# Threshold and scores compared as bfloat16 views, and the program laid out anew: sparse attention with a feed-forward block, one Trainium2 core

## The chip, the core and the metric

One core of one Trainium2 chip runs the whole program. The metric is device time in microseconds; the kernel before took 1494.7 us (median of three runs, 1494.3 to 1497.42). Engines are named as in the profile: PE (matrix multiply, PEld its weight loads), DVE (VectorE), ACT (ScalarE), POOL (GpSimd), SP (which issues DMAs).

## What is computed

```python
scores = scale * np.matmul(q, k.transpose(0, 1, 3, 2))          # 8 batches, 8 heads, 576 x 576, D = 64
kth = np.partition(scores, -32, axis=-1)[..., -32:-31]
scores = np.where(scores >= kth, scores, -1e9)                  # only the 32 largest of a row stay
attn = np.exp(scores - scores.max(-1)); attn = attn / (attn.sum(-1) + 1e-09)
out = np.matmul(attn, v)
x = out.transpose(0, 2, 1, 3).reshape(4608, 512)                # tokens x model
h = x @ w_in                                                    # 512 -> 2048
g = s * np.maximum(h, 0) ** 2 + b
return g @ w_out                                                # 2048 -> 512
```

## The kernel before

**Attention** goes by tiles of 128 query rows by 576 keys: nine tiles for each pair of heads, 32 pairs, 288 tiles. For one tile PE makes the scores in two halves (`scores`, tile `s_ps`, one buffer), ACT copies them out (`sc`), and DVE looks for the 32nd largest of each row. It takes the eight largest of each of eight groups (`groups`), picks of these (`pick`, twice), negates (`negate`, tile `nt`), and takes the eight smallest candidates (`lowest`, tile `wl`). The last of those, `wl[7]`, is minus a threshold that is a little too low. `half_at` (POOL, line 458) turns its upper 16 bits, read as an integer, into a number between two steps of the upper half; `side` (ACT, line 464) compares the upper halves of all 576 scores with it by a Sign, and counts the signs with its accumulator. `window` and `pad` (POOL, tile `wt`) let only the scores below the threshold stand and fill as many pads as are to be dropped; `wmax` (DVE, tile `chk`) then finds the exact 32nd value, and `mask` (DVE) multiplies the exponentials `e` (ACT) with the comparison. PE transposes the result (`put`, tile `tp`), ACT and DVE split it into a high and a low part (`ph`, `pl`), and PE multiplies it with the values (`attend`, tile `av`). In the first batch the values are multiplied in one piece (lines 550 and 551), later in a high and a low part (lines 554 to 556).

**Feed-forward**: 18 blocks of 256 tokens, each with 16 chunks of 128 hidden units, 288 chunks. A chunk is 12 matmuls `h` (four channel groups of three), ACT's `relu` and `square`, POOL's `ghigh` and `glow`, and six matmuls `ops`. Block 0 needs the first four tiles of all four pairs of batch 0, that is the first 16 tiles, and each later block what its tokens need.

**Weights** come in 64 steps: DVE rebuilds float32 from the 64-bit words (three operations a step, `bits0` to `bits2`), ACT and POOL split it. Until the first `h` PE fills its idle time with matmuls that nobody reads (`keep_busy`, line 383).

**What sets the order.** All of this is one graph of operations. `PARTS` gives each kind its engine, how long it holds the engine (ns), how long until its result is there, and an offset to its priority. The priority (`key`) is the tile number plus the offset; a chunk's is `TURN0 + chunk / TURNS`, a weight step's `WTURN * n / 64`. `Graph.order` takes at each step, among what could start within `SLACK` ns of the earliest on an engine, the smallest key, and the instructions are issued in the order of the starts so planned, each engine's strictly in line. The number of `keep_busy` matmuls is 0.7 of PE's planned idle time before the first `h`, by 119 ns. At the end `flag0` reduces the thresholds of all tiles to a flag: if any is not positive, a slow general path computes everything again.

Of the kernel before, what the change touches and what calls it, by code (L numbers as in the profile page):

```python
# [40 lines left out]


PARTS = {
    "wload": ("SP", 1000, 4400, 8.71), "bits0": ("DVE", 325, 420, 38.47), "bits1": ("DVE", 330, 420, 12.33), "bits2": ("DVE", 322, 412, -54.81),
    "colsum": ("PE", 7400, 7600, -52.81), "far0": ("ACT", 322, 430, 45.58), "far1": ("ACT", 507, 524, -10.00), "far2": ("ACT", 782, 793, -41.40),
    "whigh": ("ACT", 322, 425, -19.96), "wlow": ("POOL", 702, 740, -54.59), "farmax": ("DVE", 170, 250, -9.09), "bias": ("ACT", 695, 700, -15.64),
    "kqload": ("SP", 1050, 4000, -31.15), "kqhigh": ("ACT", 574, 678, -31.99), "kqlow": ("POOL", 1389, 1430, -10.46),
    "kdir": ("SP", 560, 3800, -37.66), "kdhigh": ("ACT", 574, 678, -16.79), "kdlow": ("POOL", 1389, 1430, 9.70), "kdkeep": ("SP", 1100, 3600, -26.80),
    "qdir": ("SP", 500, 3400, -28.88), "qdhigh": ("ACT", 306, 405, 40.88), "qdlow": ("POOL", 694, 736, -38.25), "mdir": ("SP", 460, 2800, -9.58), "mdhigh": ("ACT", 170, 270, -53.70), "mdlow": ("POOL", 230, 280, -38.09),
    "kqkeep": ("SP", 1000, 3900, -48.58), "kplace": ("SP", 1000, 4400, -3.60), "qplace": ("SP", 480, 3000, -15.59), "mplace": ("SP", 500, 2400, 30.78),  # L50
    "vload": ("SP", 620, 3600, -16.48), "vhigh": ("ACT", 360, 466, 2.96), "vlow": ("POOL", 838, 875, 34.45), "vkeep": ("SP", 600, 2800, 48.38),
    "qk": ("PE", 132, 300, -43.54), "sc": ("ACT", 291, 408, -37.56), "group": ("DVE", 134, 218, 60.00),
    "m1": ("DVE", 86, 173, -57.06), "m2": ("DVE", 86, 173, 0.54), "neg": ("DVE", 95, 180, -1.22), "low8": ("DVE", 94, 180, 15.04), "max": ("DVE", 72, 160, -15.68),
    "half": ("POOL", 147, 190, 44.13), "side": ("ACT", 759, 860, -18.51), "win": ("POOL", 1250, 1290, -12.54),
    "exp": ("ACT", 667, 748, 55.25), "wmax": ("DVE", 668, 754, -35.90), "pad": ("POOL", 480, 420, -5.48), "mask": ("DVE", 731, 815, -58.93),
    "put": ("PE", 436, 680, 1.41), "putq": ("PE", 108, 350, 13.37), "high": ("ACT", 478, 595, 55.65), "low": ("DVE", 590, 675, -3.19),
    "resth": ("ACT", 264, 372, 17.15), "restl": ("DVE", 568, 610, -43.14), "av": ("PE", 146, 320, -18.63), "avout": ("ACT", 320, 470, -18.43),
    "eps": ("ACT", 95, 200, -14.34), "recip": ("DVE", 72, 180, 23.03),
    "sums": ("DVE", 140, 230, 34.96), "add": ("POOL", 1375, 1420, -57.27), "spread": ("POOL", 525, 560, -55.31), "turn": ("PE", 108, 352, -31.85),
    "scale": ("DVE", 325, 405, 11.38), "xkeep": ("SP", 500, 2600, 28.44),  # L60
    "xload": ("SP", 460, 2700, -54.47), "xhigh": ("ACT", 306, 405, -24.83), "xlow": ("POOL", 694, 736, -37.81),
    "h": ("PE", 357, 523, 40.36), "relu": ("ACT", 263, 378, -60.00), "square": ("ACT", 306, 415, -27.06), "ghigh": ("POOL", 369, 405, 56.67),
    "glow": ("POOL", 705, 745, 56.08), "o": ("PE", 231, 395, 42.40), "wagain": ("SP", 920, 3900, 44.77), "flag0": ("DVE", 560, 640, 60.00), "flag1": ("PE", 110, 360, 50.77), "flag2": ("DVE", 420, 500, 23.67), "osb": ("DVE", 654, 738, -13.89), "store": ("SP", 450, 2300, -30.67),
}
# [155 lines left out]
def fast_path(ctx, tc, kq, v, w_in, w_out, s_in, b_in, out, flag):  # L220
    nc = tc.nc
# [8 lines left out]
    scale = 0.125  # L230
# [19 lines left out]
    s_col, b_col, mid, cm, tm, tx, eps = (cols[:, x : x + 1] for x in range(PADS, PADS + 7))  # L250
# [41 lines left out]
    bias = const.tile([P, DM], F32, name="bias")  # L292
# [174 lines left out]

    def window(t):
# [263 lines left out]
    for i, (b, hp, pt, order) in enumerate(plan):  # L732
        pr = Pair()
# [10 lines left out]
        for n in order:  # L744
            t = TileState()
# [324 lines left out]
    for blk in range(NBLK):  # L1070
# [16 lines left out]
        for fc in range(NFC):  # L1087
# [246 lines left out]
```

## Time and profile before

| | |
|---|---|
| median of three runs | 1494.7 us |
| the profiled execution | 1495.7 us |
| its span, first to last instruction | 1493.9 us |
| mean granted PE clock | 0.986 |
| busy: PE, PEld, DVE, ACT, POOL | 1433.2, 1263.4, 1261.7, 1283.4, 1150.9 us |
| matmuls, keep_busy among them | 9468, 203 |

Busy is the time in which an engine has at least one instruction under way. Matmuls and the operations of DVE and ACT overlap the next one's start, so the mean of one is longer than what it holds its engine for: that is read from the starts of its neighbours.

### The profile page before, as it was taken

The page shows a single profiled execution, that of the slowest core. Times are in us where ns is not written, and L with a number is a line of the kernel's source. Part 1 is how long each engine was busy: PE and PEld are TensorE (multiplying, and loading weights), DVE is VectorE, ACT ScalarE, POOL GpSimd, SP SyncE. Part 2 cuts the span into 40 slices and gives each one's busy share as a digit, 9 for nine tenths or more (in the row PEclk, how much of TensorE's full clock was granted, in tenths as well). Part 3 has the DMA queues.
Part 4 walks back from the last instruction along what each step waited for, and adds up shares of the span by engine and source line. Part 5 has one row for each costly group of instructions (what it writes and reads, how often), then busy time and mean ns, then how long its engine had stood idle before and what let it go on. Part 6 is the DMA issues. An engine that isn't in the chain of part 4 may idle for free.

```text
span 1493.9 us, 34308 instructions
## 1 busy us (share of the span) xinstructions
PE 1433.2 (96%) x9468; PEld 1263.4 (85%) x9468; DVE 1261.7 (84%) x5527; ACT 1283.4 (86%) x3382; POOL 1150.9 (77%) x1920
## 2 busy tenths in 40 slices
PE   6977999999999999999999999999999999999996
PEld 5744678999989899988898989999899989989885
DVE  6988998999999999999999999889999987875000
ACT  6777888998999899989999999888998998888366
POOL 6877887888888878888888788877888877675532
PEclk9987999999999999999999999999999999999998
DMA  6776766666566665676666665666566555552144
GB/s 184 221 204 180 221 179 172 179 177 191 159 178 195 182 171 155 187 211 174 177 195 196 170 182 163 192 175 168 157 197 185 149 176 139 145 167 87 45 151 134
DMA packets 173735, 256.63 MB, mean 172 GB/s; under 512 B 41952, under 2 KB 83936, under 8 KB 173536
## 3 DMA queue, kind: packets, MB, share of 16 engines
q1 hardware_dynamic: 173536, 254.37, 59.6%
q8 instruction: 78, 1.28, 0.4%
q14 instruction: 121, 0.99, 0.2%
HBM read 181.67 MB, written 72.61 MB: 170 GB/s over the span
## 4 chain that ended last, share of the span: by engine, by line
PE 73%; DVE 8%; ACT 8%; POOL 4%; DMA 4%; issue 2%; SPq 0%; POOLq 0%; DVEq 0%; ACTq 0%
PE ops L688 21%; PE h L665 21%; PE s_ps L418 10%; PE tp L515 7%; PE av L554 3%; PE av L555 3%; PE av L550 2%; PE tq L520 2%; DVE cand L429 1%; DVE sc L488 1%; DVE chk L484 1%; DMA kr<-in_kq_dram 1%; ACT sg L464 1%; DMA out_dram<-osb 1%; ACT sc L373 1%
## 5 line engine op out<-in xcount | busy, mean ns | idle before, releaser
L429 DVE MAX8 cand<-sc 128x8 f32<-128x72 f32 x2304 | 410.2, 221 | 37.1 <-ACT sc L424 35.7
L470 POOL TENSOR_TENSOR wt<-sc,sg 128x576 f32<-128x576 f32 x288 | 371.6, 1290 | 75.9 <-ACT sg L464 44.2
L665 PE MATMUL h<-x,wih 128*128 128x256 f32 x2176 | 427.7, 289 | 1.9 <-ACT rt L671 1.3
L665 PEld LDWEIGHTS h<-x,wih 128*128 128x128 f32 x2176 | 350.5, 190 | 21.5 <-ACT rt L671 4.6
L665 PE MATMUL h<-x,wil 128*128 128x256 f32 x1088 | 306.8, 282 | 0.0
L418 PE MATMUL s_ps<-ka,qs 128*128 128x288 f32 x1024 | 244.6, 321 | 27.9 <-ACT sc L424 11.0
L424 ACT ACTIVATE sc<-s_ps 128x288 f32<-128x288 f32 x576 | 233.5, 405 | 29.0 <-PE s_ps L418 23.8
L464 ACT ACTIVATE sg<-sc,nb 128x576 bf16<-128x576 int16 x288 | 222.5, 773 | 25.5 <-POOL nb L458 20.4
L484 DVE MAX8 chk<-wt 128x8 f32<-128x584 f32 x288 | 219.3, 761 | 23.2 <-POOL wt L474 20.8
L488 DVE SCALAR_TENSOR_TENSOR sc<-sc,chk,e 128x576 f32<-128x576 f32 x288 | 232.3, 807 | 7.4 <-ACT e L478 5.1
L478 ACT ACTIVATE e<-sc,nb 128x576 f32<-128x576 f32 x288 | 213.5, 741 | 25.7 <-DVE sc L488 18.2
L682 POOL TENSOR_TENSOR gl<-rt,gh 128x256 fp32r<-128x256 f32 x288 | 212.6, 739 | 27.3 <-PE ops L688 8.8
L418 PEld LDWEIGHTS s_ps<-ka,qs 128*128 128x128 f32 x1024 | 165.5, 193 | 70.9 <-ACT sc L424 39.0
L688 PE MATMUL ops<-woh,gh 128*128 128x512 f32 x576 | 202.3, 411 | 5.7 <-DVE osb L696 5.2
L665 PEld LDWEIGHTS h<-x,wil 128*128 128x128 f32 x1088 | 206.2, 190 | 0.0
L678 POOL TENSOR_SCALAR gh<-rt 128x256 fp32r<-128x256 f32 x288 | 116.7, 406 | 108.0 <-PE ops L688 50.3
L688 PE MATMUL ops<-woh,gl 128*128 128x512 f32 x576 | 196.3, 403 | 0.4 <-POOL gl L682 0.4
L688 PE MATMUL ops<-wol,gh 128*128 128x512 f32 x576 | 195.0, 404 | 0.0
L530 DVE TENSOR_TENSOR pl<-tp,ph 128x512 fp32r<-128x512 f32 x252 | 172.5, 684 | 23.4 <-ACT ph L525 20.4
L515 PE MATMUL tp<-idr,sc 128*128 128x128 f32 x1152 | 176.6, 276 | 3.5 <-DVE sc L488 1.6
L525 ACT ACTIVATE ph<-tp 128x512 fp32r<-128x512 f32 (+1 forms) x288 | 170.4, 592 | 5.3 <-PE tp L515 3.2
L671 ACT ACTIVATE rt<-h 128x256 f32<-128x256 f32 x288 | 109.2, 379 | 50.8 <-PE h L665 46.6
(151 smaller groups left out, 2941.5 us busy)
## 6 DMA issues: line engine op xcount, KB each, us to landing
ka<-kd SPq DMA_DIRECT2D x240, 288.0 KB, 4.4
vd<-vst SPq DMA_DIRECT2D x56, 320.0 KB, 3.9
vst<-vd SPq DMA_DIRECT2D x56, 320.0 KB, 3.2
kr<-in_kq_dram SPq DMA_DIRECT2D x56, 288.0 KB, 3.5
kd<-kh SPq DMA_DIRECT2D x56, 288.0 KB, 3.8
kd<-kr SPq DMA_DIRECT2D x56, 288.0 KB, 3.3
qs<-kd SPq DMA_DIRECT2D x224, 64.0 KB, 2.3
out_dram<-osb SPq DMA_DIRECT2D x36, 256.0 KB, 2.2
```

The source lines that it names most:

```text
L418: nc.tensor.matmul(t.ps[:, :SH], st, kx[:, cs], start=(m == 0), stop=(m == last))
L424: nc.scalar.activation(t.sc[:, hf * SH : (hf + 1) * SH], t.ps[:, :SH], AF.Identity, scale=scale)
L429: nc.vector.max(t.cand[:, g, 1:9], t.sc[:, g * GW : (g + 1) * GW])
L464: nc.scalar.activation(t.sg, t.sc.bitcast(I16)[:, 1::2], AF.Sign, bias=t.half, scale=-1.0, accum_out=t.cnt[:, 0:1])
L470: nc.gpsimd.tensor_tensor(out=t.wt[:, :S], in0=t.sc, in1=t.sg, op=ALU.mult)
L478: nc.scalar.activation(t.e, t.sc, AF.Exp, bias=t.nb)
L484: nc.vector.max(t.pair.chk[:, t.i, 0:PADS], t.wt)
L488: nc.vector.scalar_tensor_tensor(t.sc, t.sc, chk[:, PADS - 1 : PADS], t.e, op0=ALU.is_ge, op1=ALU.mult, accum_out=chk[:, PADS : PADS + 1])
L515: nc.tensor.transpose(tp[:, c, :], t.sc[:, c * P : (c + 1) * P], idf)
L665: nc.tensor.matmul(k.h, wi_at(a, cc, fc * P, P), k.x[cc][:, c, :], start=(cc == 0 and i == 0), stop=(cc == NCC - 1 and i == 2))
L682: nc.gpsimd.tensor_tensor(out=k.gl[fc], in0=k.rt[fc], in1=k.gh[fc].bitcast(F32), op=ALU.subtract)
L688: nc.tensor.matmul(k.ops[t], g[fc][:, t * P : (t + 1) * P], wo_at(w, fc, 0, DM), start=(fc == 0 and i == 0), stop=(fc == NFC - 1 and i == 2),)
```

## The change

The threshold is negated by DVE instead of shifted by POOL: `half_at` becomes a `tensor_reduce` over one element with `negate=True`, which reads the upper half of `wl[7]` as bfloat16. ACT reads the upper halves of the scores as bfloat16 too. The half step between two values, which POOL's constant 32767.5 gave, is now in the scale: -(1 + 2^-9) makes a score whose upper half equals the threshold's come out on the kept side, as before, as long as the threshold is positive. The flag tests that by `> 1.0e-30` over minima, where it tested `< 32767` over maxima.

The table has new slots and new offsets in all of its rows, and `SLACK`, `TURN0`, `TURNS` and `WTURN` are new. Instructions are the same otherwise, but for the number of `keep_busy` matmuls: 203 before, 152 now.

```diff
 PARTS = {
-    "half": ("POOL", 147, 190, 44.13), "side": ("ACT", 759, 860, -18.51), "win": ("POOL", 1250, 1290, -12.54),
+    "half": ("DVE", 62, 150, 39.94), "side": ("ACT", 759, 860, -23.40), "win": ("POOL", 1250, 1290, 9.77),
 ...
-SLACK = {"PE": 26, "DVE": 33, "ACT": 43, "POOL": 120, "SP": 861}
+SLACK = {"PE": 25, "DVE": 6, "ACT": 55, "POOL": 94, "SP": 532}
-TURN0, TURNS = 33.0, 1.074
+TURN0, TURNS = 46.3, 1.140
-WTURN = 50.4
+WTURN = 61.2
 ...
     def half_at(t):
         t.half = bias_tile(t)[:, 1, t.i : t.i + 1]
-        nc.gpsimd.tensor_scalar(t.half, t.wl.bitcast(I16)[:, 15:16], 1.0, 32767.5, op0=ALU.mult, op1=ALU.add)
+        nc.vector.tensor_reduce(t.half, t.wl.bitcast(BF16)[:, 15:16], axis=AX.X, op=ALU.max, negate=True)
 
     def side(t):
 ...
         nc.scalar.activation(
-            t.sg, t.sc.bitcast(I16)[:, 1::2], AF.Sign, bias=t.half, scale=-1.0, accum_out=t.cnt[:, 0:1]
+            t.sg, t.sc.bitcast(BF16)[:, 1::2], AF.Sign, bias=t.half, scale=-1.0 - 2.0**-9, accum_out=t.cnt[:, 0:1]
         )
 ...
-        nc.vector.tensor_reduce(tmin[:, 1, pr.i : pr.i + 1], pr.nb[:, 1, :n], axis=AX.X, op=ALU.max)
+        nc.vector.tensor_reduce(tmin[:, 1, pr.i : pr.i + 1], pr.nb[:, 1, :n], axis=AX.X, op=ALU.min)
 ...
-        nc.vector.tensor_reduce(tx, tmin[:, 1], axis=AX.X, op=ALU.max)
-        nc.vector.scalar_tensor_tensor(tm, tx, 32767.0, tm, op0=ALU.is_lt, op1=ALU.mult)
+        nc.vector.tensor_reduce(tx, tmin[:, 1], axis=AX.X, op=ALU.min)
+        nc.vector.scalar_tensor_tensor(tm, tx, 1.0e-30, tm, op0=ALU.is_gt, op1=ALU.mult)
```

Lines after the first few are numbered one lower in the new kernel. Three places show what moves.

DVE about the 101st tile, where the threshold is found, before:

```order
L453 TENSOR_REDUCE nb<-nt 128x1
L444 MAX wl<-nt 128x8
L429 MAX cand<-sc 128x8 x5
L484 MAX chk<-wt 128x8
L429 MAX cand<-sc 128x8
L488 SCALAR_TENSOR_TENSOR sc,chk<-sc,chk,e 128x576
```

and about the same tile now (`nb` is written by two lines: 452 is the row's maximum for the exponential, 457 the threshold):

```order
L483 MAX chk<-wt 128x8
L452 TENSOR_REDUCE nb<-nt 128x1
L443 MAX wl<-nt 128x8
L428 MAX cand<-sc 128x8
L457 TENSOR_REDUCE nb<-wl 128x1
L428 MAX cand<-sc 128x8
```

The threshold's operation now stands on DVE, here one short operation behind the one that it reads from. Of the 288 there are 51 with nothing between, 179 with one operation, 58 with more.

POOL at about the same tile, before:

```order
L682 TENSOR_TENSOR gl<-rt,gh 128x256
L474 TENSOR_SCALAR wt<-cols,cnt 128x8
L458 TENSOR_SCALAR nb<-wl 128x1
L678 TENSOR_SCALAR gh<-rt 128x256
L470 TENSOR_TENSOR wt<-sc,sg 128x576
```

and now:

```order
L681 TENSOR_TENSOR gl<-rt,gh 128x256
L473 TENSOR_SCALAR wt<-cols,cnt 128x8
L677 TENSOR_SCALAR gh<-rt 128x256
L681 TENSOR_TENSOR gl<-rt,gh 128x256
L469 TENSOR_TENSOR wt<-sc,sg 128x576
```

The row with `nb` is gone from POOL, and `window` follows `pad` and the feed-forward's own operations.

PE where the first chunk gets its last channel group and the first output, before (22 tiles have been transposed by `tp` ahead of the first `h` row here):

```order
L665 MATMUL h<-x,wih 128x256 x2
L665 MATMUL h<-x,wil 128x256
L418 MATMUL s_ps<-ka,qs 128x288 x2
L607 MATMUL e<-idr,avl 128x128 x2
L610 MATMUL e<-idr,ri 128x128
L520 MATMUL tq<-idr,sc 64x128
L515 MATMUL tp<-idr,sc 128x128 x4
L418 MATMUL s_ps<-ka,qs 128x288 x2
L665 MATMUL h<-x,wih 128x256 x2
L665 MATMUL h<-x,wil 128x256
```

and now (20 tiles ahead of the first row):

```order
L664 MATMUL h<-x,wih 128x256 x2
L664 MATMUL h<-x,wil 128x256
L549 MATMUL av<-ph,vst 64x320 x4
L550 MATMUL av<-p_345,vst 64x320
L514 MATMUL tp<-idr,sc 128x128 x4
L417 MATMUL s_ps<-ka,qs 128x288 x2
L664 MATMUL h<-x,wih 128x256 x2
L664 MATMUL h<-x,wil 128x256
```

The feed-forward starts two tiles earlier in the row of tiles. The very first `h`, which ends the `keep_busy` matmuls, moves more: it stood behind ten transposed tiles and stands behind seven. At the 48th tile 22.8 chunks have passed instead of 21.0, at the 96th 64.0 in both, and behind the last transposed tile 32.5 are left instead of 33.5. Weight steps end at the 40th tile in both orders.

## Rows read from the trace of the kernel before

**Rows 1.** The page: busy time of each engine, share of the span, instructions.

```profile
PE 1433.2 (96%) x9468; PEld 1263.4 (85%) x9468; DVE 1261.7 (84%) x5527; ACT 1283.4 (86%) x3382; POOL 1150.9 (77%) x1920
```

**Rows 2.** Busy time by stretch; columns in the first line.

```profile
core 0: us, PE busy (x) PEld busy (x) DVE busy (x) ACT busy (x) POOL busy (x), PEclk, DMA share, GB/s
0.00:77.00 77.00, 59.14 (x356) 47.12 (x357) 63.80 (x289) 53.75 (x133) 57.00 (x97) 1.00 0.68 203
0.00:143.00 143.00, 108.84 (x545) 75.76 (x546) 122.44 (x553) 101.94 (x253) 104.83 (x173) 0.89 0.68 198
143.00:200.00 57.00, 52.34 (x299) 38.53 (x299) 51.65 (x232) 50.42 (x129) 50.30 (x80) 0.97 0.75 216
200.00:1300.00 1100.00, 1093.13 (x7470) 988.97 (x7469) 1025.87 (x4512) 996.50 (x2573) 900.23 (x1501) 1.00 0.62 175
```

**Rows 3.** The page: the chain that ended last, by engine.

```profile
PE 73%; DVE 8%; ACT 8%; POOL 4%; DMA 4%; issue 2%; SPq 0%; POOLq 0%; DVEq 0%; ACTq 0%
```

**Rows 4.** PE in order of time, the first channel group, the last, the first output.

```profile
78.84 0.50 PE L665 MATMUL h<-x,wih 128*128 128x256 f32 x2
...
142.84 0.48 PE L665 MATMUL h<-x,wih 128*128 128x256 f32 x2
...
148.39 0.73 PE L688 MATMUL ops<-woh,gh 128*128 128x512 f32 x2 [0.52 <-POOL gh L678]
```

**Rows 5.** PE busy by stretch, transposes of line 515 alone (four a tile).

```profile
77.00:143.00 66.00, 8.97 (x48) 6.34 (x48) 0.77 0.66 191
```

**Rows 6.** Groups of instructions: busy us, mean ns of one, idle before and its releasers.

```profile
L458 POOL TENSOR_SCALAR nb<-wl 128x1 f32<-128x1 int16 x288 | 54.9, 191 | 39.3 <-DVE wl L444 17.1 <-PE tq L520 1.1
L444 DVE MAX8 wl<-nt 128x8 f32<-128x31 f32 x288 | 52.9, 184 | 0.2
L453 DVE TENSOR_REDUCE nb<-nt 128x1 f32<-128x8 f32 x288 | 42.8, 149 | 2.0
L464 ACT ACTIVATE sg<-sc,nb 128x576 bf16<-128x576 int16 x288 | 222.5, 773 | 25.5 <-POOL nb L458 20.4 <-POOL wt L470 2.9
L478 ACT ACTIVATE e<-sc,nb 128x576 f32<-128x576 f32 x288 | 213.5, 741 | 25.7 <-DVE sc L488 18.2 <-DVE avu L617 2.6 <-DVE avu L624 2.5
L342 DVE TENSOR_SCALAR ops<-wil 128x256 int32<-128x256 int32 x8 | 3.4, 423 | 0.0
```

**Rows 7.** DVE in order of time: start us, us, what.

```profile
706.31 0.16 DVE L572 TENSOR_REDUCE tmin<-chk 128x1 f32<-128x8 f32 x1
706.39 0.15 DVE L573 TENSOR_REDUCE tmin<-nb 128x1 f32<-128x4 f32 x1
...
706.80 0.18 DVE L444 MAX8 wl<-nt 128x8 f32<-128x31 f32 x1
```

**Rows 8.** POOL in order of time at the same place.

```profile
706.82 0.74 POOL L682 TENSOR_TENSOR gl<-rt,gh 128x256 fp32r<-128x256 f32 x1
707.64 0.27 POOL L474 TENSOR_SCALAR wt<-cols,cnt 128x8 f32<-128x8 f32 x1
707.99 0.19 POOL L458 TENSOR_SCALAR nb<-wl 128x1 f32<-128x1 int16 x1
```

**Rows 9.** Waits from 200 to 1300 us: in total, times, longest.

```profile
PEld s_ps L418 <- ACT sc L424: 21.0, 77, 1.3
DVE cand L429 <- ACT sc L424: 17.2, 24, 3.0
ACT sg L464 <- POOL nb L458: 17.1, 29, 1.7
DVE pl L530 <- ACT ph L525: 14.7, 24, 2.8
...
DVE chk L484 <- POOL wt L474: 11.7, 18, 2.1
```

**Rows 10.** The thresholds' readers from 200 to 1300 us, one line for the count.

```profile
L464 ACT ACTIVATE sg<-sc,nb x241: 759/776/802, 199.9 to 1296.0; 128x576 bf16<-128x576 int16 x121
```

**Rows 11.** PE in order of time, the same eight matmuls at two times.

```profile
66.29 1.94 PE L550 MATMUL av<-ph,vst 128*64 128x256 f32 x8 [0.47 <-ACT ph L525]
...
88.44 3.68 PE L550 MATMUL av<-ph,vst 128*64 128x256 f32 x8
```

More of the change, by code (lines that the diff above doesn't have):

```diff
@@ L14 @@
 I32 = mybir.dt.int32
-I16 = mybir.dt.int16
 AF = mybir.ActivationFunctionType
@@ L43 @@
 PARTS = {
[L44 to L47, printed above, removed]
@@ L48 @@
-    "kdir": ("SP", 560, 3800, -37.66), "kdhigh": ("ACT", 574, 678, -16.79), "kdlow": ("POOL", 1389, 1430, 9.70), "kdkeep": ("SP", 1100, 3600, -26.80),
-    "qdir": ("SP", 500, 3400, -28.88), "qdhigh": ("ACT", 306, 405, 40.88), "qdlow": ("POOL", 694, 736, -38.25), "mdir": ("SP", 460, 2800, -9.58), "mdhigh": ("ACT", 170, 270, -53.70), "mdlow": ("POOL", 230, 280, -38.09),
-    "kqkeep": ("SP", 1000, 3900, -48.58), "kplace": ("SP", 1000, 4400, -3.60), "qplace": ("SP", 480, 3000, -15.59), "mplace": ("SP", 500, 2400, 30.78),
@@ L51 @@
-    "vload": ("SP", 620, 3600, -16.48), "vhigh": ("ACT", 360, 466, 2.96), "vlow": ("POOL", 838, 875, 34.45), "vkeep": ("SP", 600, 2800, 48.38),
-    "qk": ("PE", 132, 300, -43.54), "sc": ("ACT", 291, 408, -37.56), "group": ("DVE", 134, 218, 60.00),
-    "m1": ("DVE", 86, 173, -57.06), "m2": ("DVE", 86, 173, 0.54), "neg": ("DVE", 95, 180, -1.22), "low8": ("DVE", 94, 180, 15.04), "max": ("DVE", 72, 160, -15.68),
-    "half": ("POOL", 147, 190, 44.13), "side": ("ACT", 759, 860, -18.51), "win": ("POOL", 1250, 1290, -12.54),
@@ L55 @@
[L55 to L63, printed above, removed]
-}
@@ L66 @@
-SLACK = {"PE": 26, "DVE": 33, "ACT": 43, "POOL": 120, "SP": 861}
-TURN0, TURNS = 33.0, 1.074
-WTURN = 50.4
+    "wload": ("SP", 1000, 4400, 25.93), "bits0": ("DVE", 325, 415, 34.13), "bits1": ("DVE", 321, 412, 12.73), "bits2": ("DVE", 321, 404, -9.12),
+    "colsum": ("PE", 7400, 7600, -55.87), "far0": ("ACT", 322, 430, 26.16), "far1": ("ACT", 507, 524, 31.42), "far2": ("ACT", 782, 793, -30.40),
+    "whigh": ("ACT", 322, 425, -28.16), "wlow": ("POOL", 700, 736, -38.79), "farmax": ("DVE", 170, 250, 2.18), "bias": ("ACT", 695, 700, -5.56),
@@ new lines @@
+    "kqload": ("SP", 1050, 4000, -30.30), "kqhigh": ("ACT", 574, 678, -24.30), "kqlow": ("POOL", 1386, 1420, 2.19),
+    "kdir": ("SP", 560, 3800, -33.57), "kdhigh": ("ACT", 574, 678, -9.36), "kdlow": ("POOL", 1373, 1410, 35.52), "kdkeep": ("SP", 1100, 3600, -17.82),
+    "qdir": ("SP", 500, 3400, -18.09), "qdhigh": ("ACT", 306, 405, 30.89), "qdlow": ("POOL", 804, 840, -58.97), "mdir": ("SP", 460, 2800, -54.12), "mdhigh": ("ACT", 170, 270, -45.01), "mdlow": ("POOL", 400, 410, -12.85),
+    "kqkeep": ("SP", 1000, 3900, -53.56), "kplace": ("SP", 1000, 4400, 3.90), "qplace": ("SP", 480, 3000, -18.42), "mplace": ("SP", 500, 2400, 12.12),
@@ new lines @@
+    "vload": ("SP", 620, 3600, -17.52), "vhigh": ("ACT", 360, 466, 11.14), "vlow": ("POOL", 840, 875, 23.08), "vkeep": ("SP", 600, 2800, 24.57),
+    "qk": ("PE", 132, 300, -56.87), "sc": ("ACT", 291, 408, -28.95), "group": ("DVE", 134, 218, 59.37),
+    "m1": ("DVE", 92, 180, -43.52), "m2": ("DVE", 93, 180, -10.28), "neg": ("DVE", 120, 203, 25.09), "low8": ("DVE", 100, 182, 17.03), "max": ("DVE", 60, 143, -17.04),
+    "half": ("DVE", 62, 150, 39.94), "side": ("ACT", 759, 860, -23.40), "win": ("POOL", 1250, 1290, 9.77),
@@ new lines @@
+    "exp": ("ACT", 667, 748, 54.55), "wmax": ("DVE", 668, 754, -30.58), "pad": ("POOL", 480, 420, 18.91), "mask": ("DVE", 724, 807, -31.31),
+    "put": ("PE", 436, 680, -29.69), "putq": ("PE", 108, 350, 8.64), "high": ("ACT", 478, 595, 42.03), "low": ("DVE", 590, 675, -9.26),
+    "resth": ("ACT", 264, 372, 21.37), "restl": ("DVE", 568, 610, -44.84), "av": ("PE", 146, 320, -53.21), "avout": ("ACT", 320, 470, 6.46),
+    "eps": ("ACT", 192, 298, -3.29), "recip": ("DVE", 78, 168, 26.19),
+    "sums": ("DVE", 125, 207, 23.53), "add": ("POOL", 1375, 1420, 11.98), "spread": ("POOL", 525, 560, -59.88), "turn": ("PE", 108, 352, -39.39),
@@ new lines @@
+    "scale": ("DVE", 325, 405, 17.95), "xkeep": ("SP", 500, 2600, 23.17),
+    "xload": ("SP", 460, 2700, -58.05), "xhigh": ("ACT", 306, 405, -17.74), "xlow": ("POOL", 692, 732, -35.39),
+    "h": ("PE", 357, 523, 39.15), "relu": ("ACT", 263, 378, -56.14), "square": ("ACT", 306, 415, -36.18), "ghigh": ("POOL", 369, 405, 60.00),
+    "glow": ("POOL", 705, 745, 53.52), "o": ("PE", 231, 395, 41.58), "wagain": ("SP", 920, 3900, 52.95), "flag0": ("DVE", 560, 640, 16.73), "flag1": ("PE", 110, 360, 11.41), "flag2": ("DVE", 420, 500, 42.48), "osb": ("DVE", 665, 750, -31.89), "store": ("SP", 450, 2300, -59.18),
+}
```

## The prediction

> **What bounds the kernel now.** I read the page's busy shares first, then the busy time by stretch, since one share over 1494 us mixes a start with another limit. PE is busy 1433.2 us, 96% of the span, the next engines 86% and 84% [rows 1], and the chain that ended last lies on PE for 73% [rows 3]. The stretches show where PE is not the limit. From 200 to 1300 us PE is idle 1100 - 1093.1 = 6.9 us; there nothing but less PE work or fewer small hitches between matmuls can win anything. In the first 143 us it is busy 108.8 [rows 2], 203 `keep_busy` matmuls among that, because the feed-forward has not begun: the first output matmul stands at 148.4 us, right after the first chunk's last channel group, which begins at 142.8 [rows 4]. So the end is set by two numbers: when PE gets enough to do, and how long the rest of PE's work takes from there.
>
> Times below are against the profiled execution's own 1495.7 us (span 1493.9 and 1.8 around it). The median of the runs, 1494.7, lies 1.0 below; I take that off at the end.
>
> **The start, moved by the new order.** The order on PE shows that channel group behind 20 transposed tiles, where it stood behind 22. What a tile takes there: from 77 to 143 us the trace has 48 transposes, 12 tiles, in 66 us [rows 5], so 5.5 us each, and two are 11.0 us.
> - Gain: -11.0 us for PE's start with chunks.
> - What PE has then not done is left for later, when PE is the limit. Its busy time from 77 to 143 was 108.84 - 59.14 = 49.7 us [rows 2], at a mean granted clock of 0.77 [rows 5]. The clock lost in that stretch is 0.23 x 66 = 15.2 us, and PE was busy 49.7 / 66 = 75% of it, so 11.4 us of the busy time are the clock's. 38.3 us for 12 tiles is 3.2 us a tile, and two tiles give back +6.4. That is the high end, since busy counts latency and matmuls overlap; the low end is nothing.
> - Weight steps: 64 in 40 tiles, so some three fewer are done by then. Three operations of 0.42 us each [rows 6] make 3.8 us on DVE. From 143 to 200 us DVE is idle 57 - 51.65 = 5.35 us [rows 2], which hides them: 0, or +3.8 if that idle time comes in the wrong places.
> - The granted clock. Until the first `h` at 78.8 us [rows 4] idle time is filled, and the profile grants full clock; then it is 0.77 until 143, and eight matmuls of line 550 take 3.68 us where they took 1.94 [rows 11]: 1.2 GHz instead of 2.4. The new order stops filling behind seven tiles instead of ten. From the last filler to the last channel group it was 10 to 22, 12 tiles, and is 7 to 20, 13. The clock's 11.4 us over 12 tiles are 0.95 a tile: +1.0.
> - The 51 fewer fillers cost nothing themselves, since they stood in idle time.
>
> The Trainium skill, "TensorE: Matmul & The Clock Gate" (section "What's actually happening"), says that the throttled state is the default and that activity releases it. By that rule the earlier end of the fillers speaks against the change: three more tiles without them would be 3 x 0.95 = 2.9 us instead of 1.0. The rows agree that the clock falls where the fillers end; they do not show which of the two counts is right, and 1.9 us would not change the forecast's side.
>
> **The threshold on DVE.** 288 POOL operations of 191 ns go, 54.9 us [rows 6]. POOL is at 900.2 of 1100 us in the steady stretch [rows 2], so that alone is worth 0. DVE gets 288 reductions over one element. The nearest row is line 453's, of the same kind, with 149 ns from start to end [rows 6]; but two neighbours of this kind start at 706.31 and 706.39 us [rows 7], so one holds DVE for about 80 ns when the next does not wait for it. Where nothing stands between it and the `wl` that it reads, 51 times, DVE waits up to 184 ns more [rows 6]. Low end 241 x 80 = 19.3 us in the steady stretch, which has 241 tiles [rows 10], and for the waits 43 of the 51 (241 / 288 of them) x 0.1 = 4.3, where 0.1 is 184 less 80 ns; together 23.6; high end 241 x 149 + 43 x 184 ns = 35.9 + 7.9 = 43.8 us.
> What covers it: DVE is idle 1100 - 1025.9 = 74.1 us there [rows 2]. Of that 17.2 + 14.7 + 11.7 = 43.6 end with something from ACT or POOL [rows 9] and can't all be used; 30.5 can. I take the low end, as the order mostly puts a short operation between: 23.6 fits, cost 0. Without that cover it is what exceeds 30.5, up to 13.3 us. In the start there is less cover: DVE is busy 122.4 of 143 us [rows 2], and 21 tiles x 80 ns = +1.7 I count in full.
>
> The Trainium skill's page "VectorE: DVE Perf Modes" (section "Rules for kernel authors") tells us to minimize the number of operations on DVE, and to expect a `tensor_reduce` to be its slowest kind. That rule speaks against moving 288 of them from the engine with most room to a fuller one. What it would do here is the rival "DVE decides" below; the rows at 706 us do not show it, as the two reductions there cost 80 ns and nothing waited.
>
> **The wait that goes.** The threshold came in POOL's line: `wl` ends at 706.98 us, POOL is in `gl` and then in `pad`, and starts the operation at 707.99 [rows 7, 8], one microsecond later. On DVE it can start at once. ACT waited for it 17.1 us in the steady stretch [rows 9], 20.4 in all [rows 6]. ACT's time is not PE's: PE's loads wait for ACT's scores 77 times [rows 9] in 2 x 241 halves, so about a sixth of ACT's delays arrive at PE: 17.1 / 6 = 2.9, -3 us. Low end 0; high end all 17.1, since PE waits for those scores 21.0 us [rows 9] and could use it. Late next is then `wt` on POOL or the maximum `chk` that waits for it.
>
> **The comparison on ACT.** It reads 16-bit values at a stride of two, before and after. The integer kind takes 773 ns where the exponential of as many float32 takes 741 [rows 6]: at best 32 ns less, 288 x 32 = 9.2 us of ACT, worth a sixth, -1.5; at worst no row shows a loss. I take 0, since the stride and the accumulator are as good a reason for the 32 ns. The flag's and `finish1`'s edits exchange one operation for its like: 0. The end: one chunk less behind the last tile is work done earlier on an engine that has no idle time to put it in: 0.
>
> Sum: -11.0 + 6.4 + 0 + 1.0 + 1.7 - 3 = -4.9; 1495.7 - 4.9 = 1490.8, less 1.0 is 1489.8. I forecast 1490, with an own range of 1485 to 1495 (the terms left over: PE's 6.4 down to 0 or so, the weight steps' 3.8).
>
> **Rivals.**
> - *The wait's end reaches PE.* ACT's 17.1 us come back by two thirds instead of a sixth, -11 instead of -3: 1482. For it: PE waits longest for just these scores. Against it: most of ACT's idle time ends for other reasons, and PE's idle time in the steady stretch is 6.9 us by the records, so the gain must lie in gaps between starts that these hide.
> - *Given back.* The two tiles are made good by the 48th tile's 1.8 more chunks and lost again by the 96th, where both orders have 64.0. If the tiles run slower as chunks run ahead, the start's gain is the 1.8 chunks at no time: 1495. For it: DVE and ACT have 7% and 9% of idle time in the steady stretch [rows 2], little to run tiles and more chunks at once. Against it: PE's total work is the same, and idle time saved is saved.
> - *DVE decides* (slower). If a reduction holds DVE for the full 149 ns and its wait, 43.8 us do not fit the 30.5 that are free; the 13.3 left show on `mask` and `pl`, for which PE waits: 1490 + 13.3, about 1503. It decides from (30.5 - 4.3) / 241 = 109 ns each. For it: DVE is the fuller engine, and planned with a slack of 6 ns instead of 33 it has less to choose from. Against it: rows at 80 ns.
> - *A longer slow start.* If the fillers' end moves three tiles and the feed-forward's start does not move in time, -11.0 and +6.4 fall away, 3 x 0.95 = 2.9 of clock and 1.7 stay, with the wait's -3 not reached in time: 1495.7 + 4.6 - 1.0, about 1499.
> - *The change doesn't do what it says.* If a tie rounds to the other side or a threshold is read as 0, the flag starts the general path and the time is far above all of these. A score equal in its upper half gives a difference of -2^-9 of itself, which float32 holds; I leave 1%.
>
> **Chances.** The forecast 0.42, the wait's end reaching PE 0.18, given back 0.13, DVE decides 0.20, a longer slow start 0.06, the last 0.01. About 0.2%, 3.0 us, is what can be told from no change here, so faster means below 1491.7 and slower above 1497.7. Of the forecast's 0.42 I put 0.27 below 1491.7 and 0.15 within. Faster: 0.27 + 0.18 = 0.45. Same: 0.15 + 0.13 = 0.28. Slower: 0.20 + 0.06 + 0.01 = 0.27. The range reaches from 1477, where the wait's high end begins to be left out, to 1506, a little beyond DVE's price.
>
> **What would show it.** The start: the first output matmul at about 138 us instead of 148.4; at 146 or later that term is wrong. The threshold: a mean of the new DVE line near 150 ns, DVE's busy time in the steady stretch up by some 20 to 30 us, and PE's idle time there still below 10. If PE has waits for DVE's `sc` or `pl` that add up to more than 10 us there, DVE decides. ACT's waits for `nb` should shrink from 17.1 to below 5; if they do and PE's rate of work in the steady stretch is unchanged, the sixth was too much. The clock: full until about 60 us, then a low stretch of about 13 tiles. The forecast is wrong in kind if the first output comes earlier and the end does not.

## The result, and the profile after

The new kernel takes 1515.8 us (median of four runs, 1511.1 to 1516.2) where the kernel before, on the same chip, takes 1495.3: ratio 1.0128, 95% interval [1.0105, 1.0151]. I forecast 1490 and at most 1506; it is slower by 20 us. The profiled execution took 1515.7 us with a span of 1513.8, 19.9 more than before.

Two lines of the page after: busy time, as in [rows 1], and the chain that ended last, as in [rows 3].

```profile
PE 1437.3 (95%) x9417; PEld 1263.7 (83%) x9417; DVE 1279.5 (85%) x5815; ACT 1285.7 (85%) x3382; POOL 1095.6 (72%) x1632
...
PE 72%; DVE 9%; DMA 6%; ACT 6%; POOL 3%; issue 3%; SPq 1%; POOLq 0%; DVEq 0%; ACTq 0%
```

Busy time by stretch after; columns as in [rows 2].

```profile
0.00:77.00 77.00, 55.23 (x297) 41.77 (x298) 61.73 (x292) 51.64 (x126) 55.14 (x85) 0.93 0.68 203
0.00:143.00 143.00, 105.64 (x517) 72.63 (x517) 122.00 (x573) 104.02 (x259) 104.90 (x155) 0.89 0.72 211
143.00:200.00 57.00, 51.34 (x285) 39.18 (x286) 53.39 (x248) 48.70 (x124) 45.11 (x66) 0.91 0.69 198
200.00:1300.00 1100.00, 1076.10 (x7281) 967.88 (x7279) 1014.55 (x4632) 979.63 (x2528) 833.31 (x1228) 1.00 0.61 173
```

In the steady stretch PE is idle 23.9 us where it was 6.9, and has done 189 matmuls fewer. DVE did not take its place: its busy time there is lower than before.

PE in order of time after, the first chunk's last channel group, the second chunk's first and second, and the first output, as in [rows 4].

```profile
128.55 0.39 PE L664 MATMUL h<-x,wih 128*128 128x256 f32 x2
...
134.05 0.78 PE L664 MATMUL h<-x,wih 128*128 128x256 f32 x2
134.62 0.41 PE L664 MATMUL h<-x,wil 128*128 128x256 f32 x1
134.97 3.40 PE L549 MATMUL av<-ph,vst 128*64 128x320 f32 x8
...
139.73 0.40 PE L664 MATMUL h<-x,wih 128*128 128x256 f32 x2
...
140.81 0.40 PE L687 MATMUL ops<-woh,gh 128*128 128x512 f32 x1
```

The channel group comes 14.3 us earlier (142.84 before; I had 11.0), behind 20 transposed tiles as I had counted. The output comes only 7.6 us earlier, at 140.8 where I had 138. In both orders the second chunk's groups stand between, and in the new one a tile times its values, 3.40 us, stands between the first and the second of these. (The new order's PE list in "The change" begins with the second chunk's first group, at 134.05, and not with the first chunk's last.)

Groups of instructions after, the new operation and the comparison that reads it, as in [rows 6].

```profile
L457 DVE TENSOR_REDUCE nb<-wl 128x1 f32<-128x1 bf16 x288 | 40.6, 141 | 1.9
...
L463 ACT ACTIVATE sg<-sc,nb 128x576 bf16<-128x576 bf16 x288 | 222.3, 772 | 13.2 <-DVE nb L457 8.3 <-POOL wt L469 3.4 <-DVE cand L428 0.2
```

Waits from 200 to 1300 us after, as in [rows 9].

```profile
PEld s_ps L417 <- ACT sc L423: 20.9, 65, 1.0
...
DVE cand L428 <- ACT sc L423: 17.4, 31, 2.1
DVE pl L529 <- ACT ph L524: 17.1, 19, 2.6
...
DVE chk L483 <- POOL wt L473: 13.8, 17, 2.5
...
ACT sg L463 <- DVE nb L457: 7.0, 13, 1.5
...
PE av L553 <- POOL vst L862: 3.9, 1, 3.9
```

ACT's wait for the threshold fell from 17.1 to 7.0 us, and the 16-bit kind of the comparison made no difference (772 against 773 ns). Neither is where 20 us went. One wait is new and long: 3.9 us of PE, once.

**Where the time went.** No view gives the next table; it is worked out from the matmul records. I counted each real matmul of the trace at its usual distance from start to start (0.119 us for an `h`, 0.233 for `ops`, 0.134 for `s_ps`, and so on; fillers at nothing). That gives the same 1315 us of work for both kernels. What the span has beyond it is PE's lost time: 178.8 us before, 198.7 after. Split by place (to chunk 13; from three chunks ahead of each of the 17 boundaries between feed-forward blocks to three behind it; the rest):

```
lost time, us    start   boundaries   between   sum
before           123.7      21.5        33.6   178.8
after            119.5      51.5        27.7   198.7
difference        -4.2     +30.0        -5.9   +19.9
```

Start and tiles gained 10 us, and 30 went at the boundaries, most of them in three: 4.4, 7.3 and 10.7 us at blocks 2, 3 and 6, against 1.7, 0.6 and 2.1 before. The split hangs a little on the prices: with each kind of matmul at the median of its own starts before (0.22 and 0.27 us for line 549's, 0.03 for `tq`) the differences are -1.6, +28.0 and -6.6. The start's gain is thus 2 to 4 us, the boundaries' loss about 30 either way.

Block 3's boundary in stretches of 5 us, after, and below it the same boundary before (columns as in [rows 2]):

```profile
400.00:405.00 5.00, 5.00 (x30) 4.09 (x29) 4.73 (x31) 4.87 (x15) 3.81 (x5) 1.00 0.79 244
405.00:410.00 5.00, 2.48 (x16) 1.87 (x14) 5.00 (x20) 2.84 (x7) 3.28 (x5) 1.00 0.76 197
410.00:415.00 5.00, 3.11 (x13) 2.81 (x14) 3.54 (x17) 2.63 (x7) 3.64 (x5) 0.52 0.48 166
415.00:420.00 5.00, 5.00 (x32) 4.77 (x33) 2.91 (x7) 4.50 (x12) 3.75 (x8) 0.80 0.01 3
```

```profile
400.00:405.00 5.00, 5.00 (x38) 4.59 (x36) 4.79 (x18) 4.97 (x14) 4.24 (x9) 1.00 0.58 164
405.00:410.00 5.00, 5.00 (x36) 4.44 (x35) 4.19 (x27) 3.57 (x11) 4.66 (x9) 1.00 0.59 147
```

PE in order of time there, after (in brackets the idle time ahead of an instruction and what ended it):

```profile
399.39 0.28 PE L664 MATMUL h<-x,wil 128*128 128x256 f32 x1
...
405.60 0.28 PE L664 MATMUL h<-x,wil 128*128 128x256 f32 x1
...
406.86 0.62 PE L687 MATMUL ops<-woh,gl 128*128 128x512 f32 x2
411.42 0.58 PE L553 MATMUL av<-ph,vst 128*128 128x256 f32 x1 [3.94 <-POOL vst L862]
...
413.51 0.63 PE L664 MATMUL h<-x,wih 128*128 128x256 f32 x2
```

399.39 is the last `h` of block 2, 405.60 the third channel group of block 3's first chunk, 413.51 the fourth: 14.1 us behind the old block's end. In between PE runs out of `ops`, and stands in line behind the product of a tile whose values are not there. No other chunk can begin, since the four groups add up in `h`, which has one buffer. So until the fourth group PE has only work of tiles to do, and that comes at the pace of the other engines: DVE is busy all of 405 to 410 us, and the chain behind the 3.94 us wait lies mostly on DVE from 403.8 to 409.1, then on POOL's `window` and `vst`. At block 6 DVE is busy 24.4 of 25 us from 645 to 670. Before, DVE is busy too (4.79 and 4.19 of 5 us), but PE has chunks to work on. There the fourth group came 6.1 us behind the old block's end at this boundary, and 5.3 to 8.2 us at boundaries 1 to 15; after, it is 14.0, 14.1 and 23.5 us at blocks 2, 3 and 6.

### The profile page after: what moved, and what is told of

Read it like the earlier page. It is cut to its first block, busy times and chain, and to the rows that moved or that the text cites. A ratio compares the mean times of both kernels' runs of the same rounds, so it can differ in the third digit from the quotient of the medians.

```text
span 1513.8 us, 34382 instructions
## 1 busy us (share of the span) xinstructions
PE 1437.3 (95%) x9417; PEld 1263.7 (83%) x9417; DVE 1279.5 (85%) x5815; ACT 1285.7 (85%) x3382; POOL 1095.6 (72%) x1632
## 4 chain that ended last, share of the span: by engine, by line
PE 72%; DVE 9%; DMA 6%; ACT 6%; POOL 3%; issue 3%; SPq 1%; POOLq 0%; DVEq 0%; ACTq 0%
PE h L664 22%; PE ops L687 21%; PE s_ps L417 10%; PE tp L514 7%; PE av L554 3%; PE av L553 3%; DMA x<-xd 2%; PE av L549 2%; DVE cand L428 2%; PE tq L519 2%; DMA kr<-in_kq_dram 1%; DVE sc L487 1%; DVE chk L483 1%; ACT sg L463 1%; DMA out_dram<-osb 1%
## 5 line engine op out<-in xcount | busy, mean ns | idle before, releaser
L428 DVE MAX8 cand<-sc 128x8 f32<-128x72 f32 x2304 | 419.5, 221 | 44.9 <-ACT sc L423 43.1
L664 PE MATMUL h<-x,wih 128*128 128x256 f32 x2176 | 433.3, 290 | 5.8 <-ACT rt L670 2.3
L664 PEld LDWEIGHTS h<-x,wih 128*128 128x128 f32 x2176 | 354.2, 191 | 27.5 <-POOL x L658 6.3
L417 PE MATMUL s_ps<-ka,qs 128*128 128x288 f32 x1024 | 244.0, 320 | 31.9 <-ACT sc L423 12.3
L463 ACT ACTIVATE sg<-sc,nb 128x576 bf16<-128x576 bf16 x288 | 222.3, 772 | 13.2 <-DVE nb L457 8.3
L529 DVE TENSOR_TENSOR pl<-tp,ph 128x512 fp32r<-128x512 f32 x252 | 172.4, 684 | 31.1 <-ACT ph L524 27.7
L514 PEld LDWEIGHTS tp<-idr,sc 128*128 128x128 f32 x1152 | 136.4, 142 | 30.1 <-issue 9.0
```

What stands on the lines that cost most here:

```text
L417: nc.tensor.matmul(t.ps[:, :SH], st, kx[:, cs], start=(m == 0), stop=(m == last))
L428: nc.vector.max(t.cand[:, g, 1:9], t.sc[:, g * GW : (g + 1) * GW])
L463: nc.scalar.activation(t.sg, t.sc.bitcast(BF16)[:, 1::2], AF.Sign, bias=t.half, scale=-1.0 - 2.0**-9, accum_out=t.cnt[:, 0:1])
L514: nc.tensor.transpose(tp[:, c, :], t.sc[:, c * P : (c + 1) * P], idf)
L664: nc.tensor.matmul(k.h, wi_at(a, cc, fc * P, P), k.x[cc][:, c, :], start=(cc == 0 and i == 0), stop=(cc == NCC - 1 and i == 2))
```

## The experiments

All runs with their ratio to the kernel before on the same chip, and the lost time of their profiled execution, counted as above; the last column names the blocks 1 to 15 whose fourth group comes 10 us or more behind the old block's end.

```
                     us      ratio [95%]               start  bound. between  late blocks
before             1495-97   1                         123.7   21.5   33.6    -
after               1515.8   1.0128 [1.0105, 1.0151]   119.5   51.5   27.7    2 3 6
e1_op_alone         1504.8   1.0044 [1.0024, 1.0064]   123.9   23.4   40.5    -
e7_load             1500.3   1.0034 [1.0021, 1.0047]   124.6   24.4   37.4    -
e2_layout_alone     1546.1   1.0323 [1.0306, 1.0340]   123.2   64.2   45.8    2 3 6
e6_op_planned       1522.8   1.0197 [1.0169, 1.0224]   120.2   57.8   27.5    3 5 6
e3_rounded          1533.5   1.0243 [1.0226, 1.0260]   140.2   43.1   33.5    -
e4_slack            1536.0   1.0274 [1.0252, 1.0295]   123.6   65.2   29.6    3 6 15
e8_turns            1533.8   1.0246 [1.0224, 1.0268]   119.6   64.6   32.9    1 3 6 15
e5_new_rounded      1556.6   1.0416 [1.0394, 1.0439]   117.2   93.1   28.8    2 3 5 15
e9_three_up         1518.0   1.0156 [1.0137, 1.0175]   118.9   53.2   27.6    2 3 6
e10_all_up          1533.1   1.0260 [1.0238, 1.0282]   124.5   56.2   30.9    2 3 6
e11_before_all_up   1506.0   1.0069 [1.0048, 1.0090]   130.4   25.4   36.0    -
e12_before_late     1533.5   1.0255 [1.0235, 1.0275]   123.1   61.5   32.0    1 3 4 5 6
e13_mdlow           1480.5   0.9883 [0.9864, 0.9901]   112.1   22.7   27.4    -
e14_xkeep           1503.9   1.0046 [1.0030, 1.0061]   122.8   34.9   28.0    -
e15_one_late        1502.7   1.0041 [1.0026, 1.0056]   126.8   29.6   27.0    6
```

**The operation and the layout, apart.** e1 is the kernel before, its order untouched, with the bfloat16 operations in place of the old ones:

```diff
-        nc.gpsimd.tensor_scalar(t.half, t.wl.bitcast(I16)[:, 15:16], 1.0, 32767.5, op0=ALU.mult, op1=ALU.add)
+        nc.vector.tensor_reduce(t.half, t.wl.bitcast(BF16)[:, 15:16], axis=AX.X, op=ALU.max, negate=True)
 ...
```

> The order of before on every engine, planned with before's table, and only the threshold's operation issued to DVE instead of POOL (with the bfloat16 reads, the scale and the flag's edit); PE's order is row for row that of before. Theory 'the order costs': the 20 us lie in the new order, so this kernel runs at 1491 to 1498 us, with DVE's busy time up by some 15 to 20 us. Rival 'DVE decides': 288 operations more on DVE cost the time, so this kernel runs at 1505 to 1517, with more waits of PE for DVE.

e2 is the new order with the old operations (the reverse edit on the new kernel).

> The order of the changed kernel, planned with its table, and only the threshold's operation issued to POOL as before (with the integer reads, the scale and the flag's test of before). 'The order costs': 1508 to 1522 us, as in the changed kernel or a little above, because the threshold gets POOL's queue back. 'DVE decides': 1492 to 1500.

e7 is the kernel before, threshold on POOL, with the reduction added on DVE into a column that nobody reads (`junk = cols[:, 15:16]`).

> Before, order and threshold unchanged (the threshold is still made by POOL), with one more DVE reduction per tile of the same form as the new one, behind the operation that makes the threshold; its result goes to a spare column that nobody reads. 'The load on DVE costs': 1502 to 1508, as the operation alone on DVE in this order (1504.8). Rival 'there the threshold came at a worse time': 1495 to 1498, since nothing that anyone waits for has moved.

The operation alone costs 6.6 us, of which its mere load on DVE explains 5.0 (0.0034 x 1496; 3.1 to 7.0 by the interval), 17 ns for each of the 288; what is left over is not clear of the noise. Both times lie between the ranges of theory and rival, so neither was right about the size. Neither makes a boundary late. The layout alone costs 48, far above its range: tiles lose as well there (45.8 between), perhaps because in the new order the old operation is in nobody's plan. The two parts do not add up, 6.6 + 48 against 20; what e1 and e2 show is that the loss at blocks 2, 3 and 6 comes with the order and not with the operation.

**Other drafts of the order.** e6 plans the reduction in the table of before:

```diff
-    "half": ("POOL", 147, 190, 44.13),
+    "half": ("DVE", 62, 150, 44.13),
 ...
```

> Before, with the threshold's operation on DVE in the program and in the plan (its row says DVE, 62 and 150 ns, and keeps its offset), so the whole order is planned anew from before's table. 'A fresh draw decides, whatever engine the operation is on': 1520 to 1545, as the two fresh draws with the operation on POOL (1533 and 1536). Rival 'with a fresh draw the operation's place counts too': if DVE is the better place, below 1515; if DVE's load hurts, above 1545.

e3 and e5 round the offsets in the tables of before and of after to whole numbers; e4 and e8 give the kernel before the new `SLACK`, or the new `TURN0`, `TURNS` and `WTURN`.

> Before, with each offset of the table rounded to a whole number and nothing else changed: the same program, the same slots, a different order. Theory 'a picked order': the order of before is an unusually good one among many of the same kind, and any new draw falls back; this kernel then runs at 1503 to 1520. Rival 'this new order is a bad one': small moves of the offsets do little, 1491 to 1500.

> The changed kernel with each offset of its table rounded to a whole number: the same operations, another order. Theory 'both orders are picked': the new order is a good one of its kind too, only less so than that of before, and a fresh draw is 15 to 40 us slower than the changed kernel: 1528 to 1556. Rival 'only before's is picked': the new order is an ordinary draw, and this one runs at 1505 to 1527.

> Before, with the SLACK values of the changed kernel and nothing else changed (DVE 6 instead of 33 ns, SP 532 instead of 861, POOL 94, ACT 55, PE 25). 'A picked order': 1503 to 1520, as for any other draw. 'This new order is a bad one', by the tighter slack: 1508 to 1516 here and 1491 to 1500 with rounded offsets; by other parts of the table: 1491 to 1500 here too.

> Before, with the TURN0, TURNS and WTURN of the changed kernel and nothing else changed: chunks and weight steps get later priorities. 'Any fresh draw falls back': 1515 to 1545. Rival 'these three carry part of the new order's good side': 1497 to 1510.

Any small change of the table draws another order for the whole program, and each of these draws was 27 to 61 us slower than the kernel before, e3 and e4 by more than forecast (1520), e5 at the upper end of its range. They lose it mostly at boundaries; e3 loses 16.5 us more in the start besides. Much of it is at boundary 16, where a block waits for the very last tiles and which the table's last column leaves out: all five draws lose some 12 to 23 us there, with the fourth group 17 to 31 us behind, where the kernel before loses less than 1, with 2.8 us. Against the kernel whose table was rounded, e3 and e5 are 2.4% and 2.8% slower: rounding alone costs either table that much.

**SP's queue.** At blocks 2, 3 and 6 the last head pair's store (`xkeep`) and the fourth load of x stand late in SP's order. SP after, in order of time, at block 3:

```profile
396.95 1.74 SPq L641 DMA_DIRECT2D x<-xd  x3
...
404.51 0.38 SPq L629 DMA_DIRECT2D xd<-avu  x1
408.07 0.34 SPq L702 DMA_DIRECT2D out_dram<-osb  x1
408.53 0.35 SPq L641 DMA_DIRECT2D x<-xd  x1
```

The data of that store were there at 395.6 (the end of `scale` on DVE); SP issues it 8.9 us later, and then waits at the output's store before it gets to the load. So I took SP's queue to be the cause. e9 moves these stores and loads up in SP's order at the three blocks, and nothing on the other engines; e10 does it for all blocks, and e11 for all blocks of the kernel before:

```diff
+    def up(res):
+        xs, keep = blocks(res)
+        for blk in (2, 3, 6):
+            i = 4 * blk + 3
+            behind(res, keep[i], deps(keep[i]))
+            behind(res, xs[i], deps(xs[i]) + xs[i - 4].new[0].ops)
+        return res
...
-    for o in graph.order(SLACK):
+    for o in up(graph.order(SLACK)):
```

> The new kernel, with the order of PE, VectorE, ScalarE and GpSimd untouched; only in the order of SP's queue, for feed-forward blocks 2, 3 and 6, the store of the last head pair's attention (xkeep) stands directly behind the scaling on DVE that it stores, and the fourth load of x (xload) directly behind the last reader of its buffer or behind that store. Theory 'block boundaries' (blocks 2, 3 and 6 wait for the fourth part of x, whose store stands 13.6, 8.9 and 8.4 us in SP's in-order queue after its data are ready): lost time at chunks 32, 48 and 96, now 4.4 + 7.3 + 10.7 = 22.4 us, falls to about 2 + 2 + 4 = 8, so 1511.6 - 14 = about 1498 to 1503 us, and the first h of the fourth channel group comes 6 to 8 us after the block before ends instead of 14.0 and 14.1, and 11 to 13 instead of 23.5. Rival 'elastic' (the chunks ran ahead of the attention anyway and the wait only moves, or DVE's load decides everywhere): 1508 or more.

> The new kernel; in SP's order every store of attention stands directly behind its scaling and every load of x directly behind what it needs, in all blocks. Theory 'block boundaries': as with three blocks, and up to 4 us less at the other boundaries: 1494 to 1503. Rival 'elastic': 1508 or more. A second rival: stores put early make SP wait for DVE with the loads of keys and queries behind them; then it is slower than the kernel with three blocks mended.

> The kernel before with the same rule for all its stores of attention and loads of x. There the fourth store is issued 2.5 to 24.8 us before the block ends at each of the boundaries 1 to 15, so theory 'block boundaries' has nothing to gain: 1493 to 1497 us, the same within 0.2%. If SP's order matters in other ways (loads of keys and queries behind waiting stores), slower by more than 3 us.

That theory fell. In e9 SP issues early, in order of time at block 3:

```profile
395.29 0.44 SPq L629 DMA_DIRECT2D xd<-avu  x1
...
397.43 1.48 SPq L641 DMA_DIRECT2D x<-xd  x3
...
399.95 0.43 SPq L641 DMA_DIRECT2D x<-xd  x1
```

but PE stops as in the new kernel, at the same instruction for the same 3.94 us:

```profile
411.83 0.39 PE L553 MATMUL av<-ph,vst 128*128 128x256 f32 x1 [3.94 <-POOL vst L862]
```

The load landed 5.0 us behind the old block's end, and the fourth group still came at 14.0, since it stands late in the lines of ACT, POOL and PE too: ACT takes this part of x up at 411.17, behind an exponential that waits for DVE, and POOL at 412.23. Moving SP's work alone is worth nothing (e9), and in all blocks it hurts, most of all in the start: 5 us of e10's loss, 6.7 of e11's, where the theory had nothing to change.

e12 is the reverse: the kernel before with store and load set back in SP's order, at blocks 1, 3, 4, 5 and 6; the other engines' orders stay.

> The kernel before with the order of the other four engines untouched; in SP's order, at blocks 1, 3, 4, 5 and 6, the last store of attention that the block needs stands one to three steps behind the third load of x, and the fourth load one to three steps behind that store, much as they stand in the new kernel at blocks 2 and 3. Theory 'block boundaries': the fourth channel group begins 11 to 15 us after the block before ends instead of 6 to 7, and each of the five boundaries loses 2.5 to 6.7 us more (what blocks 2 and 3 lose in the new kernel over the kernel before): 1495.5 + 12 to 33 = 1508 to 1528. Rival 'elastic': such a wait is made good within the next tiles: under 1500.

It cost 38 us, above its range, with 40 of lost time at boundaries. PE at block 5 in order of time, and in the last line ACT:

```profile
582.27 0.63 PE L688 MATMUL ops<-woh,gl 128*128 128x512 f32 x2
590.04 0.64 PE L520 MATMUL tq<-idr,sc 128*64 128x128 f32 x2 [7.14 <-ACT avl L564]
...
587.69 0.42 ACT L655 ACTIVATE x<-x 128x256 fp32r<-128x256 f32 x1 [7.40 <-DMA x<-xd]
```

and in stretches of 5 us, PE alone (us, busy and count, granted clock, DMA share, GB/s):

```profile
580.00:585.00 5.00, 2.90 (x20) 1.00 0.82 198
585.00:590.00 5.00, 0.00 (x0) 0.62 0.15 36
590.00:595.00 5.00, 4.96 (x28) 0.69 0.22 76
```

So one late load is enough to stop PE, and mending it is not enough when the other lines were written for a late one. The way is not that of block 3 in the new kernel, though: here ACT stands in its line in front of the load itself, DVE stands 7.27 us behind ACT, and the tiles stop with them.

**One number of the table.** The order on PE shows what e9 left. Rows between the third and the fourth group of the block's first chunk: 2, 2 and 0 before at blocks 2, 3 and 6; 10, 13 and 39 after. PE's order after, at block 3:

```
L664 MATMUL h<-x,wih 128x256 x2          third group
...
L514 MATMUL tp<-idr,sc 128x128 x4
L687 MATMUL ops<-woh,gh 128x512          last outputs of the old block
L687 MATMUL ops<-wol,gh 128x512 x2
L687 MATMUL ops<-woh,gl 128x512 x2
L553 MATMUL av<-ph,vst 128x256           a tile times its values, nine rows of this kind
...
L664 MATMUL h<-x,wih 128x256 x2          fourth group
```

Three orders were drawn from the new table, each with one number changed, and the threshold on DVE as in the new kernel in all of them. In e13 and e14 no block's fourth group is planned far behind, in e15 one, block 6's.

```diff
-    "mdlow": ("POOL", 400, 410, -12.85)
+    "mdlow": ("POOL", 400, 410, -60.00)
```

> The new kernel with one number of its table changed: the offset of mdlow (a POOL step on the keys of the mixed chunk) is -60 instead of -12.85. PE's order is that of the new kernel up to the middle of chunk 3; behind it, the fourth channel group of a block follows the third without tiles' work between them at every block, also at 2, 3 and 6. VectorE has the threshold as in the new kernel. Theory 'the order parts the channel groups' (PE runs out of work where the written order sets the fourth group of a block's first chunk 13 to 24 us behind the block before, and this costs 7 to 12 us a boundary instead of 2): the fourth group begins 5 to 9.5 us after the block before ends, the lost time at the block boundaries falls from 51.5 to 22 to 28 us, and the time to 1486 to 1496 us. Rival 'VectorE's load decides' (288 more operations on the fuller engine): 1508 or more. Rival 'the boundary's wait only moves': the lost time between the boundaries rises by as much, 1505 or more.

```diff
-    "xkeep": ("SP", 500, 2600, 23.17)
+    "xkeep": ("SP", 500, 2600, -60.00)
```

> The new kernel with another single number changed: the offset of xkeep (the store of a head pair's attention) is -60 instead of 23.17, so the planner sets it, and what hangs on it on all engines, earlier. The order has no parted channel groups either (5 to 9 us at every block). Theory 'the order parts the channel groups': lost time at the boundaries 22 to 30 us, time 1494 to 1504. Both rivals: 1508 or more.

```diff
-    "high": ("ACT", 478, 595, 42.03)
+    "high": ("ACT", 478, 595, 12.00)
```

> The new kernel with a third single number changed: the offset of high (ScalarE's copy of the transposed tile) is 12 instead of 42.03. In this order one boundary is left where the fourth channel group stands far behind, that of block 6 (about 15 us). Theory 'the order parts the channel groups': boundary 96 loses 5 to 11 us, the others 1 to 4 each, the time lies between that of the two others and that of the new kernel: 1494 to 1507. Rivals: 1508 or more.

e13 takes 1480.5 us, 1.2% faster than the kernel before, and 2.4% faster than the new kernel (0.9883 / 1.0128). Its boundaries lose 22.7 us instead of 51.5, with nothing given back between them (27.4 against 27.7), and the start 7.4 us less, which I had not expected and which is why it came out below its range. (At block 3 eleven rows still stand between the groups, a tile's values among them, but they do not wait: the fourth group comes 7.7 us behind the old block's end.) Busy time of e13 in the steady stretch:

```profile
200.00:1300.00 1100.00, 1091.33 (x7484) 991.02 (x7484) 1030.39 (x4740) 998.24 (x2601) 851.36 (x1257) 1.00 0.62 176
```

PE does 14 matmuls more there than before [rows 2], with DVE busier than in either kernel. This refutes "DVE's load decides" as the reason of the 20 us: e13 has the same 288 operations more on DVE. That PE, left with tiles alone at block 3, waits for DVE's pace is another matter, and stands. e14 and e15 came out inside their ranges of time, e14 at the upper end and with 34.9 us at its boundaries, where 22 to 30 were forecast: it has no late block, but its boundaries at 12 to 14 lose 3.9, 2.9 and 5.0 us. e15 loses 5.3 us at its late block, and more in the start.

Over boundaries 1 to 15 of all 17 kernels, the lost time goes with how far behind the old block's end the fourth group comes (correlation 0.90; ten orders of PE stand behind the 17, since e1, e7, e11 and e12 keep that of before, and e2, e9 and e10 the new one):

```
fourth group behind the old block's end   under 8   8-10   10-13   13-16   over 16 us
boundaries                                    174     49       6      13        13
mean lost time, us                            1.8    2.3     5.5     6.9      11.7
```

What stays open: the three orders of the last step differ from the new kernel's everywhere behind chunk 3 or earlier, not at these boundaries alone. No run moves the fourth group alone, on all engines, at blocks 2, 3 and 6 of the new kernel. That the late group, and not something else that the same draft does there, stops PE is argued from block 3's rows and from how the loss goes with the group's place; e12 shows it for a late load only.

## Why the prediction was wrong

- *The start's gain and the work left* (-11.0 + 6.4 + 1.0 + 1.7 = -1.9): the direction was right. Lost time in the start fell by 2 to 4 us. Within it, the first chunk's last channel group came 14.3 us earlier and the first output only 7.6, since it does not stand right behind that group: 12.3 us after it, 5.5 before. The granted clock over the first 143 us is 0.89 in both kernels, so the +1.0, and the rival of a longer slow start, have nothing to show for them.
- *What PE has not done "is left for later, when PE is the limit"*: this is the step that failed. It took for granted that behind the start the new order runs at the old one's rate, so that the work left is a number of matmuls by their length. I compared the two orders in the start and at one place of a tile, and counted chunks at the 48th and the 96th tile. The 17 places where a block waits for the attention's last head pair I did not look at, and their +30 us are more than everything in my sum. The order was there to be compared: 39 rows between two channel groups where there had been none. The prediction's own sign came true, the first output earlier and the end not: it was wrong in kind. PE's idle time in the steady stretch, which was to stay below 10 us, is 23.9.
- *The threshold on DVE, 23.6 us in 30.5 of idle time, cost 0*: mis-sized for the order of before, where the load alone measures 5.0 us (e7). In orders drawn for it, it is not to be seen between the boundaries (next point).
- *The wait that goes, -3*: ACT's wait fell to 7.0, not below 5. Between the boundaries the new kernel gains 5.9 us, threshold and new order together. The six orders planned with the threshold on DVE (after, e5, e6, e13 to e15) lose 27.0 to 28.8 us there, the four planned with it on POOL (before, e3, e4, e8) 29.6 to 33.6, which fits its sign and size; the share of the wait was not measured apart.
- *The rivals*: "given back" had it that the start's gain is lost again, but put that on tiles that run slower, and at 1495; the tiles lose less than before. "DVE decides", 1503, fits e1's 1504.8 by the number alone: e1's DVE holds 22% of the chain that ended last, 8% before, but the new kernel's chain has 9%, and PE's waits for DVE's `sc` and `pl` in its steady stretch, the sign that was named for this rival, are 4.1 us at its matmuls and 10.2 at its weight loads, against 0.2 and 6.9 before: far from 20.
- *The comparison's kind and the flag, 0*: right, 772 against 773 ns.

## What to carry to other kernels

Where a table of numbers writes the order of the whole program, a change of it is a new draw: here -2.4% to +2.8% against the kernel whose table was changed, for a few numbers or a rounding, more than any single term of the prediction. Compare the two orders at every place where one stage's first work waits for another stage's last result, by the rows that stand between two parts of one unit of work, before pricing instructions. And do not price an operation by one draw: the same threshold on DVE was 20 us slower than before in one and 17 faster in another, and its worth was to be seen only away from the boundaries, over several draws.

## What the runs showed of the hardware

PE's stops cost more than their length. After the 3.94 us wait at block 3 the granted clock was 0.52 and 0.80 in the next two stretches of 5 us (between 1.2 and 2.4 GHz), the first with 1.4 us of the stop still in it. From 411.8 to 416.9 us most matmuls of 256 columns start 0.21 us apart, where 0.12 is usual, which makes about 2 us of loss on top of the stop; then the spacing is 0.12 again. In e12 the 7.14 us stop fills the stretch with 0.62, and the next has 0.69. The Trainium skill, "TensorE: Matmul & The Clock Gate" (section "What's actually happening"), has activity release the throttle; these rows agree. A reduction over one element has a mean record of 141 ns, and added 288 times to the order of before it cost 17 ns each.
